# q of eight heads at a time in 64-row tiles, with attention's VectorE and ScalarE order laid by hand

## The chip, the cores and the metric

One core of one Trainium2 chip. The time is device microseconds (us) of that core, the median of the executions of one kernel. Every set of runs times the kernel before on the same chip beside the others.

## The reference, cut to what matters

```
xn  = layernorm(x)                        # x: 2048 tokens x 576
q   = xn @ wq                             # 576 -> 32 heads of 128
p   = softmax(q @ k^T * 128**-0.5)        # the last 512 keys; 16 key/value heads
s   = (p @ v) @ wo                        # 4096 -> 576
x1  = x + shift(gelu(xn @ w1)) @ w2       # the "short MLP", 576 -> 576 -> 576
g   = silu(x1 + gelu(layernorm(x1) @ w3) @ w4)   # 576 -> 4608 -> 576
out = x + s * g
```

## The kernel before

The 2048 tokens are four blocks of 512, each with 32 heads: 128 **head slots**. In each, TensorE does four score matmuls (one for each 128 keys), 16 value matmuls of the head before, and the five matmuls that make q for the next head. Blocks of the output product and of the short MLP are laid between them as fill. The MLP with w3 and w4 follows and already works in 64-row tiles.

```python
def stage_q(u):                               # q of ONE head, full height
    w = wq_b[(u // 4) % NWQ]
    psq = ps_pq.tile([P, QB], FP32, name="psq", tag="pq")
    for kc in range(NDC):                     # NDC = 5; the fifth chunk has only 64 real rows
        nc.tensor.matmul(psq[:, :], lhsT=w[:, kc, hh * Dh:(hh + 1) * Dh], rhs=xT_b[qb % 2][:, kc, :],
                         start=(kc == 0), stop=(kc == NDC - 1))
    with tc.high_priority(offset=HP):
        ...                                   # copy to qT: VectorE in block 0, ScalarE later

# stage_v(u, t0): 8 value matmuls into one bank, then at high priority on VectorE:
#     reciprocal of the row sums, o = po * reciprocal;   stage_t(u): o -> oT by a DMA transpose

with tc.manual_schedule(engines={SP, POOL, PE}):      # these queues follow the program
    for u in range(...):                              # VectorE and ScalarE are ordered by priority
        for i in range(4):
            stage_s(u, i)
            if i == 0:
                stage_q(u + 1)                        # q of the next head
                for fn in fill.get(u, []): fn()       # layernorm steps, loads
                continue
            if i < 3: stage_v(u - 1, 2 * (i - 1))
            for fn in cut[i - 1]: fn()                # output product, short MLP
        stage_t(u - 1)
...
with tc.issue_after(last_t[0].ins):                   # the MLP's weights, behind the last oT
    for i in range(NSL): load_w(i)
...
load_sx(0)                                            # reloads s, which the output product stores
```

The kernel's pools give the attention stage eight PSUM banks: scores 3, q 2 (`pq`), values 2 (`po`, two token tiles in each), output product and short MLP 1 (`wo`).

## Time and profile before

| | before |
|---|---|
| median of its four runs beside the changed kernel | 854.61 us (851.21 to 864.56) |
| profiled run: span, mean granted TensorE clock | 847.5 us, 0.999 |
| TensorE, VectorE, ScalarE busy | 98%, 50%, 54% |
| up to block 1; block 1; block 2; block 3 with the last output product; MLP | 115.1; 133.8; 134.3; 170.7; 293.7 us |

One more view, the table of waits, gives what TensorE waited for (us in total, how often, the longest). The first line here is its only one on attention's value banks, the second its largest on q's input:

```profile
PE po L382 <- DVE o L387: 2.0, 1, 2.0
...
PE psq L350 <- DMA xT_b<-xn_b: 0.4, 1, 0.4
```

The order in which TensorE works hides nearly everything: normalization, copies, DMA transposes and loads all end in time. Of the 543.4 us from the first q to the MLP, 4.5 are idle by the prediction's count of starts.

### The profile page before, as it was taken

The page shows a single profiled execution, that of the slowest core. Times are in us where ns is not written, and L with a number is a line of the kernel's source. Part 1 is how long each engine was busy: PE and PEld are TensorE (multiplying, and loading weights), DVE is VectorE, ACT ScalarE, POOL GpSimd, SP SyncE. Part 2 cuts the span into 40 slices and gives each one's busy share as a digit, 9 for nine tenths or more (in the row PEclk, how much of TensorE's full clock was granted, in tenths as well). Part 3 has the DMA queues.
Part 4 walks back from the last instruction along what each step waited for, and adds up shares of the span by engine and source line. Part 5 has one row for each costly group of instructions (what it writes and reads, how often), then busy time and mean ns, then how long its engine had stood idle before and what let it go on. Part 6 is the DMA issues. An engine that isn't in the chain of part 4 may idle for free.

```text
span 847.5 us, 19375 instructions
## 1 busy us (share of the span) xinstructions
PE 826.8 (98%) x7896; PEld 485.0 (57%) x7980; DVE 427.7 (50%) x1351; ACT 460.9 (54%) x825; POOL 76.9 (9%) x134
## 2 busy tenths in 40 slices
PE   8999899999999999999999999999999999999996
PEld 5665555665564565565566565455555555555555
DVE  5778841267751166762154884052247537635324
ACT  5776763598793388784379874132333333334610
POOL 3441200310010111010001100000000000000000
PEclk9999999999999999999999999999999999999999
DMA  7996751473372174363048336992003301310101
GB/s 181 234 234 159 157 97 41 117 125 91 87 136 43 41 130 99 91 126 82 19 82 164 70 79 105 307 342 47 2 2 74 99 2 43 69 64 15 44 15 46
DMA packets 139983, 83.94 MB, mean 99 GB/s; under 512 B 106944, under 2 KB 133248, under 8 KB 139888
## 3 DMA queue, kind: packets, MB, share of 16 engines
q1 hardware_dynamic: 130048, 53.01, 30.6%
q0 software_dynamic: 8448, 28.15, 11.8%
q10 hardware_dynamic: 1392, 1.48, 0.5%
q8 instruction: 64, 1.05, 0.5%
q14 instruction: 31, 0.25, 0.1%
HBM read 49.17 MB, written 9.44 MB: 69 GB/s over the span
## 4 chain that ended last, share of the span: by engine, by line

## 5 line engine op out<-in xcount | busy, mean ns | idle before, releaser
L367 ACT ACTIVATE pT<-sc 128x512 bf16<-128x512 f32 x512 | 290.3, 596 | 103.5 <-PE sc L365 91.4
L365 PE MATMUL sc<-qT,kT 128*128 128x512 bf16 x493 | 175.1, 378 | 1.3 <-DVE qT L355 0.6
L382 PEld LDWEIGHTS <-pT 128*128 128x128 bf16 x2048 | 139.5, 98 | 52.9 <-DVE o L387 2.5
L382 PE MATMUL po<-v_sb,pT 128*128 128x129 bf16 x2048 | 161.4, 220 | 3.2 <-DVE o L387 2.0
L350 PE MATMUL psq<-xT_b,wq_b 128*128 128x512 bf16 x603 | 151.9, 379 | 2.5 <-DMA xT_b<-xn_b 0.4
L386 DVE RECIPROCAL ri_b<-po 128x2 f32<-128x2 f32 x256 | 43.0, 168 | 189.3 <-PE po L382 185.3
L731 PE MATMUL ph<-xT_b,w_s 64*128 64x512 bf16 x976 | 127.1, 376 | 2.3 <-DVE fence L721 2.1
L768 PE MATMUL pm<-w_s,h 64*128 64x512 bf16 x864 | 122.2, 377 | 0.9 <-DVE fence L721 0.9
L406 PE MATMUL pswo<-wo_sb,oT 128*128 128x512 bf16 x497 | 114.2, 379 | 0.8
L387 DVE TENSOR_TENSOR o<-po,ri_b 128x256 bf16<-128x256 f32 x256 | 107.9, 422 | 10.7 <-DMA oT<-o 4.3
L749 ACT ACTIVATE h<-ph 128x512 bf16<-128x512 f32 x67 | 39.4, 597 | 133.9 <-PE ph L731 133.9
L350 PEld LDWEIGHTS <-wq_b 128*128 128x128 bf16 x640 | 62.4, 98 | 74.4 <-issue 2.2
L768 PEld LDWEIGHTS <-h 64*128 64x128 bf16 x1728 | 70.8, 94 | 56.7 <-issue 1.6
L406 PEld LDWEIGHTS <-oT 128*128 128x128 bf16 x1024 | 64.9, 98 | 55.2
L768 PE MATMUL pr<-w_s,h 64*128 64x64 bf16 x864 | 90.2, 189 | 0.2 <-ACT h L749 0.2
L731 PEld LDWEIGHTS <-w_s 64*128 64x128 bf16 x1152 | 57.3, 94 | 51.0 <-issue 2.8
L357 ACT ACTIVATE qT<-psq 128x512 bf16<-128x512 f32 x96 | 57.4, 598 | 28.1 <-PE psq L350 26.7
L747 DVE COPY hx<-ph 128x512 f32<-128x512 f32 x55 | 38.0, 692 | 67.8 <-PE ph L731 67.8
L365 PEld LDWEIGHTS <-kT 128*128 128x128 bf16 x512 | 47.4, 97 | 28.4 <-DVE qT L355 1.2
L227 POOL DMA_DIRECT2D wq_b<-in_A_wq_dram x30 | 23.4, 780 | 314.4 <-PE psq L350 295.4
L721 DVE TENSOR_SCALAR fence<-ph,ph 1x1 f32<-1x1 f32 x61 | 12.6, 206 | 53.9 <-PE ph L731 53.4
L749 ACT ACTIVATE h<-hx 128x512 bf16<-128x512 f32 x55 | 34.6, 630 | 8.5 <-DVE hx L747 7.0
(114 smaller groups left out, 641.3 us busy)
## 6 DMA issues: line engine op xcount, KB each, us to landing
wq_b<-in_A_wq_dram POOLq DMA_DIRECT2D x30, 512.0 KB, 5.3
w_s<-in_B_w_dram SPq DMA_DIRECT2D x9, 576.0 KB, 7.0
wo_sb<-in_A_wo_dram POOLq DMA_DIRECT2D x8, 576.0 KB, 5.0
w_s<-in_B_w_dram SPq DMA_DIRECT2D x9, 512.0 KB, 7.9
x_dram<-x SPq DMA_DIRECT2D x4, 576.0 KB, 3.5
x<-x_dram SPq DMA_DIRECT2D x4, 576.0 KB, 5.1
s_b<-s_dram SPq DMA_DIRECT2D x4, 576.0 KB, 5.4
x_b<-in_A_x_dram SPq DMA_DIRECT2D x4, 576.0 KB, 6.6
```

What stands on the lines that cost most here:

```text
L350: nc.tensor.matmul(psq[:, :], lhsT=w[:, kc, hh * Dh:(hh + 1) * Dh], rhs=xT_b[qb % 2][:, kc, :], start=(kc == 0), stop=(kc == NDC - 1))
L357: nc.scalar.activation(out=qT[:, :], in_=psq[:, :], func=ACT.Copy)
L365: nc.tensor.matmul(sc[:, :], lhsT=kT[:, g, kc * P:(kc + 1) * P], rhs=qT_t[u][:, :], start=True, stop=True)
L367: nc.scalar.activation(out=pT[:, :], in_=sc[:, :], func=ACT.Exp, scale=SCALE)
L382: nc.tensor.matmul(po[:, j, :], lhsT=pTs[kc][:, tt * P:(tt + 1) * P], rhs=v_sb[:, g, kc, 0:Dh + 1], start=(kc == 0), stop=(kc == KCH - 1))
L386: nc.vector.reciprocal(out=ri, in_=po[:, :, Dh])
L387: nc.vector.tensor_tensor(out=o[:, t0:t0 + 2, :], in0=po[:, :, 0:Dh], in1=ri.unsqueeze(2).to_broadcast([P, 2, Dh]), op=ALU.mult)
L406: nc.tensor.matmul(ps, lhsT=oT_t[qb * Hq + h][:, tt, :], rhs=wo_sb[:, h, lo:hi], start=(h == 0), stop=(h == Hq - 1))
L731: nc.tensor.matmul(ps[i][:, :], lhsT=lhsT, rhs=xT[half, kc, :], start=first, stop=last, skip_group_check=True)
L747: nc.vector.tensor_copy(out=src[:, :], in_=ps[i][:, :])
L749: nc.scalar.activation(out=h3[:, :], in_=src[:, :], func=ACT.Gelu_apprx_tanh)
L768: nc.tensor.matmul(out, lhsT=h3_t[b, fc][half, tt * P:(tt + 1) * P], rhs=w4_s[fc // WS][half, fc % WS, lo:hi], start=key not in started, s ...
```

## The change

Its intent is to save TensorE slots. The contraction of q is 576 = 4.5 x 128, so the fifth matmul of a head is half empty. A pair of 64-row matmuls takes one slot of 0.2155 us: in the MLP of the kernel before, four pairs take 0.87 us (600.90 to 601.77). So two heads side by side in two 64-row tiles take nine slots instead of ten. A pair takes two banks here. Eight heads (four pairs) are made in one burst, which borrows the two value banks as well. Three other things come with it: VectorE and ScalarE now follow the program's order in attention, the values of a head are spread half a slot later, and x is normalized in place.

```diff
+        def stage_qs(u0, n):                                  # n = 8 heads
+            pend = None
+            for i in range(n // 2 + 1):
+                nxt = None
+                if i < n // 2:                                # first half of pair i: 5 slots
+                    psp, tag = ((ps_pq, "pq"), (ps_po, "po"))[(n // 2 - 1 - i) % 2 if u0 else i % 2]
+                    nxt = (u0 + 2 * i, [psp.tile([P, QB], FP32, name="psq", tag=tag) for _ in range(2)])
+                    q_half(xT, *nxt, [(kc, ((0, LO), (1, HI))) for kc in range(NDC)], True)
+                    f = small.tile([1, 1], FP32, name="fence")
+                    nc.vector.tensor_scalar(...)              # fence: reads both banks
+                if pend:                                      # second half of pair i - 1: 4 slots
+                    u, ps = pend
+                    q_half(xT, u, ps, [(kc, ((1, LO), (0, HI))) for kc in range(NF)], False)
+                    nc.scalar.activation(out=qT_t[u][:, :], in_=ps[0][:, :], func=ACT.Copy)
+                    nc.vector.tensor_copy(out=qT_t[u + 1][:, :], in_=ps[1][:, :])
+                pend = nxt
 ...
-            with tc.high_priority(offset=HP):
-                nc.vector.reciprocal(out=ri, in_=po[:, :, Dh])
+            nc.vector.reciprocal(out=ri, in_=po[:, :, Dh])
 ...
-            later(base + 7, lambda b=b: ln2_steps(b), 3)
+            later(base + (1 if b else 4), lambda b=b: ln2_steps(b), 5 if b else 2)
 ...
-        for j in range(2, NB * 8):
-            at(4 * (j - 1) - 1, lambda j=j: load_wq(j))
+        for j in range(3, NB * 8):
+            at(8 * (j // 2 - 1) + 1 + j % 2 if j > 3 else 4, lambda j=j: load_wq(j))
 ...
-        with tc.manual_schedule(engines={SP, POOL, PE}):
+        with tc.manual_schedule(engines={SP, POOL, PE, DVE, ACTE}):
 ...
+                if u == 4:
+                    stage_qs(4, 4)
+                elif u % 8 == 0 and 0 < u < U:
+                    stage_qs(u, 8)
                 for i in range(4):
                     stage_s(u, i)
+                    for fn in fill.get((u, i), []):           # layernorm steps stand BEFORE
+                        fn()
+                    v, tt = (u - 2, 2 + i) if i < 2 else (u - 1, i - 2)
+                    stage_v(v, tt)                            # the values and their normalization
```

(Cut: the layernorm split into steps, in place; the end of the range check moved into the MLP; the short MLP at other heads.)

## The prediction

> **What bounds the kernel now.** I read the page first, then the groups by line, the chain of waits, and the order of time in three places. The chain that ended last is empty in this trace, so the bound has to be shown by counting.
>
> ```profile
> PE 826.8 (98%) x7896; PEld 485.0 (57%) x7980; DVE 427.7 (50%) x1351; ACT 460.9 (54%) x825; POOL 76.9 (9%) x134
> ...
> L350 PE MATMUL psq<-xT_b,wq_b 128*128 128x512 bf16 x603 | 151.9, 379 | 2.5 <-DMA xT_b<-xn_b 0.4
> ```
>
> TensorE's 98% alone says little (ends of matmuls are modelled), so I count starts. Matmuls of 512 columns start 0.2155 us apart, a row of 8 value matmuls takes 0.47 us (0.0587 each), 64-column ones start 0.03 us apart. Attention (with its q, first MLP layers and output product) from the first q at 10.4 to the first MLP matmul at 553.8 us has 640 q, 512 score, 512 output, 100 and 80 short-MLP matmuls of 512 columns (1844 x 0.2155 = 397.4), 2048 value matmuls (120.2), 592 of 64 columns (17.8) and 64 transposes (3.5): 538.9 us of the 543.4. So TensorE's order of starts is full; 4.5 us are idle. A gain can only come from fewer slots. What hides behind TensorE is seen in an ordinary head:
>
> ```profile
> 375.47 0.38 PE L365 MATMUL sc<-qT,kT 128*128 128x512 bf16 x1
> ...
> 375.68 0.63 PE L382 MATMUL po<-v_sb,pT 128*128 128x129 bf16 x8
> ...
> 376.15 0.38 PE L365 MATMUL sc<-qT,kT 128*128 128x512 bf16 x1
> ...
> 376.35 0.17 DVE L386 RECIPROCAL ri_b<-po 128x2 f32<-128x2 f32 x1 [1.56 <-PE po L382]
> 376.37 0.63 PE L382 MATMUL po<-v_sb,pT 128*128 128x129 bf16 x8
> 376.56 0.42 DVE L387 TENSOR_TENSOR o<-po,ri_b 128x256 bf16<-128x256 f32 x1
> 376.84 0.59 PE L365 MATMUL sc<-qT,kT 128*128 128x512 bf16 x2
> ...
> 377.27 1.24 PE L350 MATMUL psq<-xT_b,wq_b 128*128 128x512 bf16 x5
> 378.35 0.38 PE L365 MATMUL sc<-qT,kT 128*128 128x512 bf16 x1
> ...
> 378.55 0.60 ACT L357 ACTIVATE qT<-psq 128x512 bf16<-128x512 f32 x1 [0.21 <-PE psq L350]
> ```
>
> A head takes 378.35 - 375.47 = 2.88 us: 4 scores 0.86, 16 values 0.94, 5 q matmuls 1.08. VectorE waits 1.56 us between heads. ScalarE's four exps start 0.478 to 0.494 us apart when they run back to back and one q copy adds about 0.5: some 2.45 us of 2.88. The last line gives a latency that I use below: the fifth q matmul starts at 377.27 + 4 x 0.2155 = 378.13, its copy at 378.55, 0.42 later. VectorE's copy of q (first block) takes 0.69, and a matmul waiting for it starts 0.05 after its end.
>
> [...] the MLP leaves its 64-row tiles: the last eight begin at 804.45, so the next slot is due at 805.31; it starts at 805.43, about 0.1 us late. [...]
>
> **The change, part by part.**
>
> *Slots removed.* The contraction of 576 is four and a half chunks of 128; before, the half chunk took a whole slot. Now two heads take 5 + 4 slots of paired 64-row matmuls instead of 10. The MLP's pairs, eight matmuls in four slots (600.90 to 601.77), show that a pair costs one slot. 64 x 0.2155 = **-13.8 us**.
>
> *Banks within a burst.* Eight heads are four pairs P0 to P3, in the order P0 first half, P1 first, P0 second, P2 first, P1 second, P3 first, P2 second, P3 second. There are only four banks: P0 and P2 share the value banks, P1 and P3 the q banks. P2's first half comes straight after P0's second[...]. It must wait for both copies of P0: from the last slot's start 0.42 to the copy, 0.69 for VectorE's, 0.05 back, 1.16, less the slot of 0.2155: 0.94 us idle. The same before P3. The MLP has the same turn of banks and covers it with other work:
>
> ```profile
> 600.90 1.04 PE L731 MATMUL ph<-xT_b,w_s 64*128 64x512 bf16 x8
> 601.77 0.40 PE L768 MATMUL pm<-w_s,h 64*128 64x512 bf16 x2
> ...
> 602.03 0.69 DVE L747 COPY hx<-ph 128x512 f32<-128x512 f32 x1 [1.68 <-PE ph L731]
> ...
> 602.72 0.21 PE L768 MATMUL pr<-w_s,h 64*128 64x64 bf16 x2
> ...
> 602.78 1.04 PE L731 MATMUL ph<-xT_b,w_s 64*128 64x512 bf16 x8
> ```
>
> There, 1.0 us of down-projection lies between the last use of the bank and the next. In the q burst nothing lies there. A burst of eight is thus 36 x 0.2155 + 2 x 0.94 = 9.64 us where eight single heads took 8.62: longer, not shorter. There are 15 bursts of eight (the first eight heads go in two fours without such a turn): 30 x 0.94 = **+28.2 us**.
>
> *Entry of a burst.* P0 takes both value banks just after the last value matmuls. The second bank is free 0.2 + 0.21 + 0.42 + 0.05 = 0.88 us after them. Where two matmuls of the short MLP stand in between (about six of 16 entries) 0.45 remain. 10 x 0.85 + 6 x 0.45 = **+11 us**. *Mode changes*: 17 bursts at 0.1 to 0.15: **+2 us**.
>
> *ScalarE.* With q gone from the heads, a head without other fill is 1.80 us of TensorE against 4 x 0.485 = 1.94 of exps. Heads with fill and bursts let ScalarE catch up, and three score banks and values half a slot later allow about 1 us of lag, so only long runs without fill show it: **+2 us**.
>
> *VectorE order.* Before, value normalization had priority over layernorm. Now VectorE follows the program, and four or five layernorm steps stand ahead of a head's normalization. Statistics of four tiles took 3.85 us at the start of the trace (3.71 to 7.56). With only two value banks TensorE can go on for about one head. Second layernorm, blocks 1 to 3, five steps in the second slot: counted from the end of the burst, VectorE is free at 2.8 us (two heads at 1.9, less what waits), statistics and the start of the inverse root (4.05) hold it to 6.85, the normalization ends at about 7.2 instead of 3.5, and TensorE, which wants its bank at 4.1, stops for 3.0 us: 3 x 3 = 9. Next block's layernorm, blocks 1 and 2: 3.0 + 1.3 + 1.2 = 5.5 each: 11. Block 0, where GELU, k copies and layernorm coincide, 6; last one 2.5. Sum 28.5; I take 24, since VectorE overlaps neighbours a little and fill may hide some. **+24 us**.
>
> *Idle that goes away*: the 4.5 us counted above are absorbed by the new waits: **-4.5**. Normalizing x in place removes buffers and memsets that lie beside other work: 0. The flag's end moved into the MLP: 0.
>
> Sum: -13.8 + 28.2 + 11 + 2 + 2 + 24 - 4.5 = +48.9 us.
>
> **The rivals.** (1) *The slots are simply saved*: all turns of banks are hidden, 857.6 - 13.8 - 4.5 = about 839. For it: TensorE is full now, and the MLP gains from the same tiles. Against: there, the turn is covered by a microsecond of other matmuls, here by nothing. (2) *Only the burst's own waits cost*: VectorE's order is harmless, because the sparse heads have slack (VectorE idle 1.56 us of 2.88). Then -13.8 + 28.2 + 11 + 2 - 4.5 = +23, about 881. For it: the author laid the order by hand and would have looked. Against: without q a head has 1.8 to 1.94 us, and 3.85 us of statistics cannot fit ahead of its normalization. (3) *ScalarE becomes the bound*: every head at 1.94 or more and q bursts in series, which adds up to 0.14 x 18 heads x 4 = 10 us to what is above, about 915. Against: slots with fill are TensorE-bound and let it catch up.
>
> **Range and chances.** The profiled run took 849.25 us, the median of three 857.6; adding 48.9 gives 898 and 906, and I take 902. The low end, 872, is the burst's waits alone with small entries; the high end, 928, has VectorE's order in full and rival 3. That the result is within 2% (below 874.8) needs both the entries and VectorE's order to cost almost nothing: 0.08. Faster by over 2% needs the first rival and more than all idle time: 0.03.
>
> **What would show it.** In the changed profile: q matmuls in runs of 18 with pauses of about 0.9 us ended by the qT copies, twice in a burst; a burst of eight near 10 us; waits of TensorE for VectorE's normalization (o) of 2 to 3 us in the second and 25th heads of a block; heads without fill of 1.8 to 2.0 us; MLP stage unchanged near 294 us. Wrong would be: bursts near 7.8 us (banks free in time), or no wait for o beyond the entries.

## The result, and the profile after

| | before | after |
|---|---|---|
| median | 854.61 us (851.21 to 864.56, 4 runs) | 978.39 us (974.77 to 981.18, 4 runs) |
| ratio of fast runs | 1 | 1.1429 (95%: 1.1341 to 1.1517) |
| profiled run: span, granted clock | 847.5 us, 0.999 | 979.4 us, 0.968 |

A ratio here and below is the ratio of fast runs to those of the kernel before in the same rounds; it is not quite the ratio of the medians quoted. The change costs 123.8 us by the medians. (One of the four runs before, 864.56, lies 1.6% above the fastest; without it the median is 851.61, and the cost 126.8.) The prediction had +48.9 and a range up to 928 us: the direction was right, the size far off.

**Where.** Lengths between the starts of blocks, in the two traces:

| | up to block 1 | block 1 | block 2 | block 3 + output | wait for MLP weights | MLP |
|---|---|---|---|---|---|---|
| before | 115.1 | 133.8 | 134.3 | 170.7 | 0 | 293.7 |
| after | 162.2 | 159.8 | 160.2 | 191.5 | 12.4 | 293.4 |

(Some 7.5 us of the first column is q of seven more heads of block 1, which the burst makes before the block's first score.) Every part of attention loses; the MLP is untouched, as predicted. The page of the changed kernel, first its busy shares, then the granted clock in 40 slices (tenths), then its value matmuls (count, busy us and mean ns, idle time before them and what ended it):

```profile
PE 862.5 (88%) x8492; PEld 498.2 (51%) x8492; DVE 476.9 (49%) x1463; ACT 435.5 (44%) x793; POOL 90.3 (9%) x160
...
PEclk9987899999999999999999999998899999999999
...
L396 PE MATMUL po<-v_sb,pT 128*128 128x129 bf16 x2048 | 207.0, 224 | 43.3 <-DVE o L403 43.3
```

TensorE fell from 98% to 88%, and its granted clock sags to 0.7 or 0.8 in slices 3 to 5 and to 0.8 in slices 28 and 29. The table of waits names the causes:

```profile
PE po L396 <- DVE o L403: 43.3, 37, 3.3
PE psq L371 <- ACT qT L362: 20.8, 30, 0.7
PE psq L371 <- DVE o L403: 13.9, 6, 10.2
PE ph L735 <- DMA w_s<-in_B_w_dram: 12.4, 1, 12.4
PE psx L526 <- DVE x L536: 6.9, 11, 2.5
...
PE pswo L423 <- ACT x L433: 2.1, 9, 0.2
```

Such a line counts from the modelled end of the matmul before, which lies some 0.17 us after the next one was due (a matmul of 512 columns is shown with 0.38 to 0.39 us, and the next starts 0.2155 after it). I therefore counted again by starts: how much later than its slot each matmul begins, with the slots of the prediction and half slots for the 64-row ones, from 10.4 us to the MLP.

| cause of the lateness | us |
|---|---|
| value matmuls wait for VectorE's o | 49.4 |
| q waits for the copies of its banks (30 turns) | 28.8 |
| q waits for o (one pause of 10.25, and true entries) | 16 |
| TensorE at half clock after pauses (granted 0.50 to 0.70 in the stretches that follow them) | some 14 |
| MLP weights | 12.5 |
| short MLP waits for its residual add | 8.7 |
| first score after a burst (16 times 0.20) | 3.2 |
| output product waits for its bank's copy | 4.8 |
| other scores: waits for exps (2.5 of them in four places) and small delays | some 5 |
| DMA transposes of xn, rest | some 4 |

The sum is about 146. Less 13.8 of slots saved and less the 4.5 that were idle before, this makes 128 of the 131.9 us of span. Some 4 us I did not assign.

**A burst.** The order of time around one burst (start, duration, in brackets the idle time before and what ended it):

```profile
247.24 3.55 PE L371 MATMUL psq<-xT_b,wq_b 64*128 64x512 bf16 x28
...
250.83 0.60 ACT L362 ACTIVATE qT<-psq 128x512 bf16<-128x512 f32 x1 [3.55 <-PE psq L371]
251.48 2.12 PE L371 MATMUL psq<-xT_b,wq_b 64*128 64x512 bf16 x18 [0.69 <-ACT qT L362]
...
254.30 3.03 PE L371 MATMUL psq<-xT_b,wq_b 64*128 64x512 bf16 x26 [0.70 <-ACT qT L362]
...
257.26 0.39 PE L379 MATMUL sc<-qT,kT 128*128 128x512 bf16 x1
```

Two pauses, each ended by ScalarE's copy: the 18 matmuls from 251.48 are nine slots, so the next was due at 253.42 and came 0.88 later. The burst lasts 257.26 - 247.24 = 10.02 us, where eight single heads took 8.62.

**VectorE in the second head of a block** (block 1). Four statistics stand ahead of the normalization for which TensorE waits:

```profile
164.80 0.81 DVE L137 BATCH_NORM_STATS2 ln_st<-xn_b 128x6 f32<-128x288 bf16 x2
...
168.42 0.21 DVE L138 BATCH_NORM_AGGREGATE ln_mv<-ln_st 128x2 f32<-128x12 f32 x1
...
169.14 0.42 DVE L403 TENSOR_TENSOR o<-po,ri_b 128x256 bf16<-128x256 f32 x1
...
169.62 0.62 PE L396 MATMUL po<-v_sb,pT 128*128 128x129 bf16 x4 [3.31 <-DVE o L403]
...
170.03 3.31 PE L423 MATMUL pswo<-wo_sb,oT 128*128 128x512 bf16 x8
...
173.63 1.89 PE L423 MATMUL pswo<-wo_sb,oT 128*128 128x512 bf16 x8
```

The pause of 3.31 us is what the prediction worked out (3.0). What it left out is in the last two lines: eight matmuls of the output product take 3.31 us right after the pause (the same figure by chance), and the next eight such in a row take 1.89 us. The granted clock from 168 to 174 us was 0.72.

**The longest pause** lies at head 15 of block 0. The first line is the issue of a DMA transpose of o on SyncE's queue:

```profile
66.48 8.07 SPq L412 DMA_TRANSPOSE oT<-o  x1
...
78.83 0.42 DVE L403 TENSOR_TENSOR o<-po,ri_b 128x256 bf16<-128x256 f32 x1 [10.21 <-DMA oT<-o]
...
79.31 5.56 PE L371 MATMUL psq<-xT_b,wq_b 64*128 64x512 bf16 x27 [10.25 <-DVE o L403]
```

VectorE waits 10.21 us because a buffer of o is still being transposed, and TensorE waits for VectorE. In this stretch (56 to 95 us) transposes of o needed 5.6 us in the median and up to 20.7 us to land, while the loads of the first block came together. From 60 to 82 us the packets of the load queue took 64.9% of the time of the core's 16 DMA engines, and those of the queue with the transposes 51.3%. Between 200 and 400 us the median is 2.5, and in the first block of the kernel before (30 to 95 us) they needed 5.9 and at most 8.9.

**The MLP's weights**, on SyncE's queue, after and then before:

```profile
673.69 0.38 SPq L705 DMA_DIRECT2D s_b<-s_dram  x1
...
675.27 1.65 SPq L690 DMA_DIRECT2D w_s<-in_B_w_dram  x1
...
686.03 1.89 PE L735 MATMUL ph<-xT_b,w_s 64*128 64x512 bf16 x8 [12.37 <-DMA w_s<-in_B_w_dram]
```

```profile
525.83 0.46 SPq L685 DMA_DIRECT2D w_s<-in_B_w_dram  x1
```

Before, the weights start 28 us ahead of the first MLP matmul (553.8). After, the reload of s stands ahead of them in the queue. It went only once the last output product was done, and the weights behind it waited, so TensorE was idle for 12.4 us. The table of waits gives SyncE's wait for that output matmul as 25.6 us.

### The profile page after: what moved, and what is told of

The parts are those of the page before. It is cut to its first block, busy times and chain, and to the rows that moved or that the text cites. A ratio compares the mean times of both kernels' runs of the same rounds, so it can differ in the third digit from the quotient of the medians.

```text
span 979.4 us, 20583 instructions
## 1 busy us (share of the span) xinstructions
PE 862.5 (88%) x8492; PEld 498.2 (51%) x8492; DVE 476.9 (49%) x1463; ACT 435.5 (44%) x793; POOL 90.3 (9%) x160
## 4 chain that ended last, share of the span: by engine, by line
## 5 line engine op out<-in xcount | busy, mean ns | idle before, releaser
L381 ACT ACTIVATE pT<-sc 128x512 bf16<-128x512 f32 x512 | 275.4, 635 | 136.2 <-PE sc L379 131.9
L396 PE MATMUL po<-v_sb,pT 128*128 128x129 bf16 x2048 | 207.0, 224 | 43.3 <-DVE o L403 43.3
L396 PEld LDWEIGHTS <-pT 128*128 128x128 bf16 x2048 | 158.9, 99 | 136.3 <-DVE o L403 57.2
L379 PE MATMUL sc<-qT,kT 128*128 128x512 bf16 x512 | 197.4, 386 | 2.1 <-ACT pT L381 1.9
L371 PE MATMUL psq<-xT_b,wq_b 64*128 64x512 bf16 x1152 | 141.1, 381 | 37.4 <-ACT qT L362 20.8
L735 PE MATMUL ph<-xT_b,w_s 64*128 64x512 bf16 x976 | 128.7, 380 | 12.6 <-DMA w_s<-in_B_w_dram 12.4
L423 PE MATMUL pswo<-wo_sb,oT 128*128 128x512 bf16 x512 | 123.1, 388 | 3.2 <-ACT x L433 2.1
L371 PEld LDWEIGHTS <-wq_b 64*128 64x128 bf16 x1152 | 68.8, 95 | 105.7 <-issue 41.3
L362 ACT ACTIVATE qT<-psq 128x512 bf16<-128x512 f32 x64 | 38.2, 597 | 144.9 <-PE psq L371 144.9
L735 PEld LDWEIGHTS <-w_s 64*128 64x128 bf16 x1152 | 58.1, 95 | 62.6 <-DMA w_s<-in_B_w_dram 12.5
L379 PEld LDWEIGHTS <-kT 128*128 128x128 bf16 x512 | 50.7, 99 | 25.4 <-issue 14.4
L363 DVE CAST qT<-psq 128x512 bf16<-128x512 f32 x64 | 44.3, 691 | 29.6 <-PE psq L371 29.6
```

Source lines behind the costliest of these rows:

```text
L362: nc.scalar.activation(out=qT_t[u][:, :], in_=ps[0][:, :], func=ACT.Copy)
L363: nc.vector.tensor_copy(out=qT_t[u + 1][:, :], in_=ps[1][:, :])
L371: nc.tensor.matmul(ps[k][:, :], lhsT=w[half, kc, hh * Dh:(hh + 1) * Dh], rhs=xT[half, kc, :], start=(first and kc == 0), stop=(not first a ...
L379: nc.tensor.matmul(sc[:, :], lhsT=kT[:, g, kc * P:(kc + 1) * P], rhs=qT_t[u][:, :], start=True, stop=True)
L381: nc.scalar.activation(out=pT[:, :], in_=sc[:, :], func=ACT.Exp, scale=SCALE)
L396: nc.tensor.matmul(po[:, j, :], lhsT=pTs[kc][:, tt * P:(tt + 1) * P], rhs=v_sb[:, g, kc, 0:Dh + 1], start=(kc == 0), stop=(kc == KCH - 1))
```

## The experiments

The theory after reading: the mechanism of the prediction holds, but q of each head had also been the cover behind which other waits were hidden, and three further parts of the change (order, queue, loads) each add their own. The rivals were that one cause, above all the burst's banks, carries nearly all; that TensorE's changes into the 64-row tiles and out again cost much; or that ScalarE is the bound. Times are medians; each ratio is to the kernel before of the same rounds (medians 853.38 for the first four runs, 855.92 for the next four, 856.38 for the last four). Differences from the changed kernel are taken from 978.4. Every run gave correct results. The intervals of e8 and e11 lie above 1 but cross 1.02, so by the 2% rule their verdict is "unclear"; e10 is the "same" as before, and all others are slower.

### e1_burst: the order of pairs within a burst

```diff
-            for i in range(n // 2 + 1):    # P0f P1f P0s P2f P1s P3f P2s P3s
+            for i in range(0, n // 2, 2):  # P0f P1f P0s P1s P2f P3f P2s P3s
+                two = [begin(i), begin(i + 1)]
+                for nxt in two:
+                    end(*nxt)
```

> Only the order of the halves within a burst of q changes: P0 and P1 first halves, then P0 and P1 second halves, then P2 and P3 in the same way, so that a pair of other matmuls lies between the last use of a bank and its next. Theory (TensorE pays the bank turn, 30 times about 0.9 us, 28.8 us by my count of starts): the waits of q for the qT copies fall from 20.8 us of shown idle to under 3, a burst of eight from 10.0 to about 8.2 us, the run from 978 to 950 to 958. Rival (what is saved in the burst is only waited for later, at VectorE's normalization or ScalarE's exps): bursts shorten, but the run stays at 970 or above.

Measured 952.84 us (ratio 1.1154, 1.1111 to 1.1197): -25.5. Every bank now turns under four slots of the other pair. The order of time shows a whole burst without a pause:

```profile
236.70 8.30 PE L378 MATMUL psq<-xT_b,wq_b 64*128 64x512 bf16 x72
244.93 0.39 PE L386 MATMUL sc<-qT,kT 128*128 128x512 bf16 x1
```

It takes 8.23 us instead of 10.02, and 15 x 1.79 = 27. (The 0.47 us beyond its 36 slots, 7.76, lie at its ends. The second matmul starts 0.25 late, which no line of TensorE's waits shows; in the changed kernel's trace its weight load, at 247.60, is put down to a wait of 0.27 for VectorE's o. The first score comes 0.20 late.) The copies' turn is thus a real cost of the size predicted (28.2), and can be avoided at no cost. It is a fifth of the whole, so the rival of one cause falls.

### e2_sched: VectorE and ScalarE ordered by priority again

```diff
-        with tc.manual_schedule(engines={SP, POOL, PE, DVE, ACTE}):
+        with tc.manual_schedule(engines={SP, POOL, PE}):
 ...                       # and around o, the q copies and fence, k copy, GELU, residual adds:
+            with tc.high_priority(offset=HP):
```

> The changed kernel, but VectorE and ScalarE in attention ordered as before by the scheduler with priority for value normalization, q copies, GELU and residual adds. Theory (the hand-laid order puts layernorm and GELU steps ahead of normalization: value matmuls lose 49 us, residual adds 9[...]): 915 to 940 us, with waits of value matmuls for o under 15 us in the sum of starts and the clock near 0.98. Rival (two value banks are too few for heads of 1.9 us whatever the order): less than 15 us gained, 963 or above.

Measured 943.69 us (1.1062, 1.1029 to 1.1096): -34.7, a miss by 4 us of the 915 to 940 that I had expected. The first line of the waits above (43.3 us, 37 times) becomes:

```profile
PE po L402 <- DVE o L410: 5.4, 8, 2.2
```

So the hand-laid order causes nearly all waits of the values. Not all of it is gained: q's wait for the DMA transposes of xn grew from 2 to 7 us.

### e3_weights: the reload of s behind the weights

```diff
-        load_sx(0)
+        with tc.issue_after(last_w.ins):
+            load_sx(0)
```

> Only the load of s and x for the last stage is put behind the MLP weights in the SyncE queue. Theory (the weights stand behind a load of s that waits for the last output matmul at 673.7): TensorE's wait of 12.4 us at the start of the MLP and the half clock after it (about 3 us) go, 961 to 966 us. Rival (the weights' memory itself is freed only by the last output matmul): they start no earlier, the run stays within 3 us of 978.

Measured 964.81 us (1.1313, 1.1285 to 1.1342): -13.6. TensorE's wait for the weights is gone from the table. Why the reload came to stand first in the queue, no run here shows; the lines that issue it and the weights are the same in both kernels.

### e4_wo_late: loads of wo later in block 0

```diff
-            at(4 + 3 * i, lambda i=i: late(pT_t[4 + 3 * i][0][0:1, 0:1], lambda: load_wo(i)))
+            at(17 + 2 * i, lambda i=i: late(pT_t[17 + 2 * i][0][0:1, 0:1], lambda: load_wo(i)))
```

> Only the eight loads of wo move from heads 4 to 25 of the first block (every third) to heads 17 to 31 (every second). Theory (loads are tied to head numbers, heads are now 1.9 us instead of 2.9, so k, v, two wq chunks and wo fall together at 55 to 70 us and the o transposes land after up to 20.7 us instead of 2.4; TensorE then waits 2.6 and 10.3 us and falls to half clock): both pauses and 4 to 6 us of half clock go, 958 to 964 us. Rival (the transposes are late because of their place in the SyncE queue behind those of the second layernorm): the pauses stay, within 4 us of 978.

Measured 977.12 us (1.1429, 1.1377 to 1.148): no gain, and my expectation fell. The rival's number came true; whether its reason did, e6 tests. The pauses at head 15 stayed (3.9 and 8.1 us). Two chunks of wq, k, v and the next x still came together between 51 and 62 us.

### e6_loads: wo, x and the last k apart

```diff
-                ux, u1 = (8, 19) if b == 0 else (base + 22, base + 24)
+                ux, u1 = (5, 19) if b == 0 else (base + 22, base + 24)
 ...
-        at(12, lambda: load_k(3))
+        at(17, lambda: load_k(3))          # and wo as in e4
```

> The changed kernel with its first-block loads taken apart further: wo at heads 17 to 31, x of the next block at head 5 instead of 8, the last k load at head 17 instead of 12, so that only wq and v remain between heads 9 and 16. Theory (the o transposes land late there because load traffic shares the DMA engines with them; moving wo alone left wq, k, v and x together): waits of 8 to 10 and 3 to 4 us near the 16th head go, with some half clock, 958 to 966 us. Rival (the transposes slow each other: o and second-layernorm transposes alternate on the SyncE queue): at least 8 us of that wait stay, 972 or above.

Measured 964.46 us (1.1272, 1.123 to 1.1315): -13.9. Of q's 13.9 us for o, with its pause of 10.2, this is left:

```profile
PE psq L371 <- DVE o L403: 4.2, 6, 2.0
```

The loads of block 0 are tied to head numbers. Where they fell close together they held up the transposes of o (up to 20.7 us to land), and those held TensorE (10.2 us, now 2.0 at most). The place of the transposes in SyncE's queue was left alone, so the rival falls. They are still slow to land (5.5 us in the median, up to 14.3 between 56 and 95 us), but the long pause is gone. The true entries of a burst are these 4.2 us as shown (some 6 by starts).

### e5_single_q: the changed kernel with q of one head at a time

```diff
-                if u == 4:
-                    stage_qs(4, 4)
-                elif u % 8 == 0 and 0 < u < U:
-                    stage_qs(u, 8)
                 for i in range(4):
                     stage_s(u, i)
+                    if i == 0 and u + 1 < U:
+                        stage_q(u + 1)     # and its loads of wq, as before the change
```

> The changed kernel with q as before: one head at a time, full-height matmuls, between the scores; hand-laid order, values half a slot later, x in place and all else stay. Theory (the burst costs through its bank turns 29, entries and exits about 20, and through the shorter heads it leaves, which VectorE's order and the loads can't follow; the hand-laid order alone costs less because a head is 2.9 us again): 880 to 900 us, value matmuls wait for o 15 to 30 us in all, the weights' wait of 12 us stays. Rival (the hand-laid order is the harm whatever q does): 925 or above. Second rival (the order is harmless at 2.9 us a head): below 872.

Measured 894.56 us (1.0457, 1.0416 to 1.0497). Bursts (with their loads of wq) account for 978.4 - 894.6 = 83.8 of the 123.8 us; order, queue and loads for 40. But the bank turns (e1: 25.5) and the loads that e6 mends (13.9, which other loads of wq may mend too) come to some 40, and this kernel even has the 13.8 us of slots back. The rest of the 83.8, I infer, is waits that q of a single head hides; e10 tests it. The waits of the values for o are 13.2 us here, just below the 15 to 30 expected. And close loads did harm with heads of 2.88 us too: once, at head 17 of block 0, the short MLP waited 9.2 us for a transpose of its input, which with the loads apart (e11) it did not.

### e7_all_sched: e1, e2, e3 and e6 together

```diff
+            for i in range(0, n // 2, 2):                      # e1
+        with tc.manual_schedule(engines={SP, POOL, PE}):       # e2
+        with tc.issue_after(last_w.ins):                       # e3
+        at(17, lambda: load_k(3))                              # e6
```

> Four mends at once: burst order, scheduler's order for VectorE and ScalarE, weights first, loads apart. If the gains measured alone add (25.5 + 34.7 + 13.6, and up to 15 for the loads): 890 to 905 us. Theory of separate causes: within 8 us of that sum. Rival (they hide each other, and a shared limit such as two value banks or 1.9 us heads stays): above 915. Still slower than before in either case, since bursts give 13.8 us and pay entries, exits and shorter cover.

Measured 892.42 us (1.0441, 1.0399 to 1.0483). The four gains add up: 978.4 - 25.5 - 34.7 - 13.6 - 13.9 = 890.7. The four causes are therefore separate, as far as the sums show. Yet with the slots saved and all four mended, the kernel is still 36.5 us behind the one before. What TensorE waits for now:

```profile
PE psx L545 <- DVE x L556: 7.3, 11, 2.9
PE psq L384 <- DMA xT_b<-xn_b: 6.7, 2, 3.7
PE psq L384 <- DVE o L417: 6.3, 7, 3.0
PE psq L384 <- DVE fence L362: 4.8, 7, 1.2
```

Four waits of 5 to 7 us each: the residual add, the transposed input, the entry and the fence.

### e10_single_mended: the same three mendings, q of one head at a time

```diff
-                elif u % 8 == 0 and 0 < u < U:                 # e7 without bursts
-                    stage_qs(u, 8)
+                    if i == 0 and u + 1 < U:
+                        stage_q(u + 1)
```

> As e7 (scheduler's order, weights first, loads apart), but q one head at a time at full height. It differs from e7 in q alone, and has 13.8 us more of matmul slots. Theory (the single heads' q was the cover under which bank turns, exps and copies went; bursts take it away even when they are mended): 853 to 862, some 30 to 38 us faster than e7 despite more slots. Rival (what is left in e7 comes from other parts of the change: half-slot values, x in place, double loads of wq): 875 or above.

Measured 856.53 us (1.0000, 0.9957 to 1.0043): as fast as before. It differs from e7 in q alone (with its loads of wq), has 13.8 us more of matmul slots, and is 36 us faster. Only two lines of its table of waits on attention's banks exceed 2 us:

```profile
PE po L385 <- DVE o L393: 4.0, 3, 3.6
PE psx L521 <- DVE x L532: 3.5, 1, 3.5
```

The residual add stopped e7 eleven times. The ten short stops (0.44 us each) are gone here; the long one stays (2.9 us in e7, 3.5 here). This is the direct evidence that q of each head was the cover: 1.08 us of work in every head, which needs only a bank of its own, and under which turns of other banks end. It also shows that values half a slot later and x in place, with the loads moved, together cost nothing measurable. The loads of wq went back with q in this run; no run changes them alone.

### e11_single_hand: e10 with the hand-laid order

```diff
+        with tc.manual_schedule(engines={SP, POOL, PE, DVE, ACTE}):    # e10 without e2
```

> As e10, but VectorE and ScalarE in the hand-laid order of the change. Theory (with heads of 2.9 us the hand-laid order costs only what its bunches of layernorm exceed: about 16 us of waits for o by the sums of the single-q run): 866 to 878. Rival (the order is free once weights and loads are mended): within 5 us of e10.

Measured 871.88 us (1.0196, 1.0158 to 1.0233). The hand-laid order costs 871.9 - 856.5 = 15 us where heads have 2.88 us, and 34.7 (e2) where they have 1.8 to 2.0. So the same VectorE work did more harm where TensorE had less to do in a head.

### e8_half_pair: the kernel before, with only the half chunks paired

```diff
+            for k, u in enumerate(us):                 # two heads, four full chunks each
+                for kc in range(NF):
+                    nc.tensor.matmul(ps[k][:, :], lhsT=w[:, kc, ...], rhs=xT[:, kc, :], ...)
+            for k, half in enumerate((LO, HI)):        # one slot for both half chunks
+                nc.tensor.matmul(ps[k][:, :], lhsT=w[half, NF, ...], rhs=xT[half, NF, :], ...)
```

> The kernel before with one thing of the change: two heads' q together, their eight full chunks at full height and only the two half chunks as one pair of 64-row matmuls, every second head. It saves 64 slots of 0.2155 us (13.8 us) and makes 128 changes of tiling mode. From the bursts' entries and exits I estimate 0.09 and 0.16 us, 0.25 a pair: 64 x (0.25 - 0.2155) = +2 us, plus 2 to 4 us of q banks shared with the short MLP: 853 to 862, no gain. Rival (a mode change is nearly free): 838 to 845, faster than before.

Measured 871.16 us (1.0174, 1.0126 to 1.0221), a miss (its three fast runs alone have a median of 869.01); its profiled run was slow (882.48 us, with a pause of 9.1 us for a late transpose of o), so only what repeats in it is read. One pair of heads:

```profile
248.06 1.89 PE L352 MATMUL psq<-xT_b,wq_b 128*128 128x512 bf16 x8
249.88 0.39 PE L356 MATMUL psq<-xT_b,wq_b 64*128 64x512 bf16 x2
250.21 0.39 PE L372 MATMUL sc<-qT,kT 128*128 128x512 bf16 x1
```

Eight slots from 248.06 end at 249.78; the pair starts at 249.88, 0.10 late. The next score is due at 250.095 and starts at 250.21, 0.115 late. Together 0.21 us for the way into the tiles and out again, and one saved slot is 0.2155, so the two cancel. That rules out a gain from this form, and also the rival of costly changes of tile: 17 bursts x 0.21 = 3.7 us of the whole. I put the loss down to the bunching: without fill, two heads take 3.95 + 2.05 = 6.00 us, where two of before take 5.76, and the head without q has less to hide its waits. No run separates this from the other small waits of that trace.

### e9_spread: layernorm steps spread over a head

```diff
-                at(u + i // per, step)
+                at(u + i // per, step, (i % per) * 4 // per)
```

> The changed kernel with one line changed: the four or five layernorm steps of a head stand at its four places instead of all at the first. Theory (it is the bunch of statistics ahead of one normalization that stops the value matmuls, not the hand-laid order as such): the 3.3 us and 2.8 us waits after layernorm shrink to about 1 us each, the waits of value matmuls for o fall from 49 to about 25 us with some half clock, 950 to 962 us. Rival (VectorE has simply more work in these heads than they last, wherever the steps stand): less than 8 us gained, 970 or above.

Measured 968.0 us (1.1302, 1.1251 to 1.1353): -10.4, between what the two theories had expected. The pauses of 3.31 us at a block's second head became 1.95, and those of 2.84 us at head 25 became two of 0.99 and 1.31. Spreading relieves the worst pile-ups; most waits remain (36.8 us shown in 39 places, after 43.3 in 37), as VectorE still takes all layernorm work within a few heads.

### e12_all_hand: everything mended, but in the hand-laid order

```diff
+        with tc.manual_schedule(engines={SP, POOL, PE, DVE, ACTE}):    # with e1, e3, e6, e9
```

> The changed kernel as its author meant it, bursts and hand-laid order kept, with burst order, spread layernorm steps, weights first and loads apart. Theory (causes add: 25.5 + 13.6 + 13.9 + 16 to 28 for the spread): 897 to 910. Rival (the spread gives little, the hand order needs the priority of normalization): 915 or above.

Measured 914.35 us (1.0701, 1.0646 to 1.0755), 4 us above what I had expected, since e9 gains so little: TensorE still waits 35.5 us for o in 39 places. Against e7, a spread hand-laid order is 21.9 us slower than the ordering by priority.

No version beat the kernel before; the best, e10, equals it.

## Why the prediction was wrong

Its own steps, with what was measured (starts in the trace of the changed kernel, or the run that undoes the part):

| step of the prediction | predicted | measured |
|---|---|---|
| slots removed | -13.8 | a pair of half matmuls takes one slot (four pairs in 0.87 us): -13.8 stands |
| banks within a burst | +28.2 | 30 turns of 0.88 in the burst shown: 26 (28.8 if half slots are counted); e1: 25.5 |
| entry of a burst | +11 | some 6, and 0.25 in each of seven bursts for which no wait is shown |
| mode changes | +2 | 0.21 per two changes (e8): 3.7 for 17 bursts; in the bursts' own trace the first scores are 3.2 late |
| ScalarE | +2 | 2.5 in four places, some 5 with small delays |
| VectorE order | +24 | 49.4 by starts; e2: 34.7 |
| idle that goes away | -4.5 | taken over as counted, not measured |
| left out: weights behind the reload of s | 0 | 12.5; e3: 13.6 |
| left out: block 0's loads delay the transposes of o | 0 | e6: 13.9 |
| left out: half clock after pauses | 0 | some 14; not undone alone |
| left out: turns of the single `wo` bank (residual add 8.7, output copy 4.8) | 0 | 13.5 |

The rows overlap (e2, e3 and e6 contain some of the half clock), so the last column is not a sum.

**What held.** The burst's bank turn was right in kind and size. One detail was not: I had VectorE's copy of 0.69 us as the last, but the release is put down to ScalarE's, shorter (0.60) and started up to 0.21 us later. The two nearly cancel. Heads without fill or pauses took 1.80 to 1.96 us (predicted 1.8 to 2.0), bursts 10.02 us (9.64 and an entry), and the MLP 293.4 us.

**The mis-sized term: VectorE's order.** The pauses that I worked out are there. The second layernorm in blocks 1 to 3 shows 3 x 3.31 = 9.9 us (predicted 9), the next block's layernorm 8.8 (11), the last one 3.8 (2.5), block 0 without its pause for loads 10.1 (6): 32.6 against 28.5. Missing in the sum are GELU, whose VectorE steps stop the values for 0.66 us at heads 11, 13 and 15 of three blocks (5.9), the shift at head 18 (1.9), a pause of 2.6 that belongs to the loads, and some 0.4 elsewhere: 43.3, the first line of the waits. The 37 late starts add 0.16 each, 6.1 us, because a wait is shown from the modelled end. I then took 24 instead of 28.5, "since VectorE overlaps neighbours a little and fill may hide some". Of the first, the trace shows 0.08 us between two neighbours (an aggregate of 0.21 from 165.64, the next statistics from 165.77), of the second nothing in these pauses: that choice went the wrong way.

**The step that failed: what was left out of the sum.** I wrote that "TensorE's order of starts is full" and that "A gain can only come from fewer slots", and from then on treated q only as slots to be counted. All else that lay hidden stayed out of the sum, as though it would stay hidden. The last four lines of the table came out once q left the heads or the queues changed. e7 and e10 show it most plainly: two kernels alike but for q and its loads of wq, the one with more matmul work 36 us faster. The single `wo` bank is the clearest case. Before, its copy or residual add ended while the next head's five q matmuls ran; in the sparse heads TensorE is back at the bank 0.2 to 0.4 us too soon, and again for each tile.

**The half clock** compounds each of these. In the trace of the changed kernel each of the ten pauses of 2.17 us or more was followed by some microseconds at half clock: in the 1.5 to 5.6 us from its end the granted clock was 0.50 to 0.70. After 2.84 us (295.30), TensorE took 0.63 us instead of 0.38 per score within 0.9 us of its return; after 1.65 us (104.17) and 1.87 us (123.53) the granted clock was 1.00. So the pause of 3.31 us in the second head cost a further 1.42 us (3.31 - 1.89). This is what one trace shows; no run varies the length of a pause alone, and I draw no limit from it. The split between pauses and the clock that they bring stays a count from the trace: no run holds the clock and keeps the pauses.

**The loads** were readable from the diff and the trace of before and I did not look: how many fall within a few heads once heads get shorter and wq comes two chunks at a time. That the reload of s would come to stand ahead of the MLP's weights was not: the diff leaves its lines alone. Of the rivals, the first (slots simply saved) and third (ScalarE) are ruled out; the second ended a little below the prediction and so further off.

What stays open: why the reload of s was put ahead of the weights; and what makes up the 36 us of e7 over e10. As e7 has 13.8 us less of slots, its waits must be some 50 us longer. The four lines shown come to 25 us, and e10 has 3.7 of these too, so less than half is named by them, and the fence, entries and transposes were not undone one by one. Nor were the loads of wq, two chunks at a time: in e7 none was issued between 252.4 and 268.7 us, when TensorE waited 2.9 us for late transposes of xn, so there at least the loads are not the likely cause.

## What to carry to other kernels

Before moving work out of a loop that keeps an engine full, list what ends under that work (bank turns, copies, normalizations, transposes) and ask for each whether something else will still cover it; here a matmul slot saved by pairing was worth 0.2155 us per pair, and one uncovered bank turn cost 0.88 us, four times that. Inside a burst, order the pairs so that each bank is copied while another pair runs (e1: -25.5 us). With engines laid by hand, put work that nothing waits for soon behind the work that TensorE waits for (e2: -34.7 us), and a transfer whose source is late behind an urgent one of the same queue (e3: -13.6 us).
